# Weight rows of 4 KB, mode groups at given iterations, and the last modes sent to their rows by transfers, in an attention and spectral-mixing kernel

## The chip, the cores and the metric

The kernel runs on one core of one Trainium2 chip. The metric is the device time of one execution in microseconds (us), as the median of several runs. In the profile PE is the matrix engine TensorE (PEld its weight load), DVE is VectorE, ACT is ScalarE, POOL is GpSimd, and SP is SyncE, which here only issues transfers. DMA stands for the core's 16 DMA engines.

## What is computed

The reference has two parts, cut here to what matters (8 batches, 8 heads, 576 positions, head size 64; then 8 x 576 x 512, 64 modes):

```python
def phi(x):                                  # q and k, with w_phi (64 x 128)
    proj = x @ w_phi
    proj = proj - max(abs(proj))
    return concat([exp(proj), exp(-proj)])
kv, z = k_p^T v, sum(k_p)
x = (q_p kv) / (q_p z + 1e-06)               # per batch and head; then [8, 576, 512]

X = rfft(x, axis=1)[:, :64]                  # 64 modes
Yr = Xr @ w_r[m] - Xi @ w_i[m]               # one 512 x 512 pair of matrices per mode
Yi = Xr @ w_i[m] + Xi @ w_r[m]
u = x + irfft(Y, n=576)
out = u + relu(u @ w_ch)
```

w_r and w_i are f32, 64 x 512 x 512 each, 134 MB together. They are by far the largest input.

## The kernel before

**Two stages of work, one stream of weights.** An attention loop runs n = 0 to 33. Its 32 states S[n] are each one pair of heads of one batch (the first eight: one head of two batches). Iteration n does the feature products of state n, the kv product and the quotient of state n-1 (`kv_mm`, `num_mm`, `numer`) and the forward transform of state n-2 (`x_mm`, line 344). A second loop (line 785 on) finishes the modes, and an output phase (line 821 on) adds the inverse transform, the residual and the relu, and stores.

**Mode groups.** The weights come in 32 groups of equal size: 8 groups of 16 modes with 64 of the 512 input rows each (gi < 0 in `groups`, line 108 on), then for each of three further head pairs g = 1 to 3 eight groups of 8 modes with 128 input rows (gi = 0 to 7). `weights(k)` (line 156) issues the transfers of group k from POOL; they cast f32 to bf16 on the way. For gi >= 0 there are two, wr and wi, each 128 partitions by 8 rows of 512 elements, so a row is 2,048 bytes read and 1,024 written. For gi < 0 there are four of 64 partitions. The pool `pw` holds three buffers of each, so group k + 3 is issued once group k has been used (NW = 3).

**Order on POOL.** In an iteration POOL runs, in program order: the transfers of q and k for later states (`load_qk`, odd n), the weights of the next group, then `vscale` (line 266), which multiplies v by exponentials that ACT made (`ee`); in n < 4 vscale comes ahead. POOL also builds `ident_f` at n = 10. Each transfer that POOL issues carries one of eight completion semaphores in turn (110 to 117 in the trace). SP loads v.

**Using a group.** `mode_mm(k)` (line 390) multiplies 16 times: for two parts ri, two parities of the mode and four j it takes 32 columns of `XT`, which holds the transformed x with blocks of zeros beside it, so that even and odd modes land in different rows of one result. `mode_sum` (line 424) adds the result to `Yacc`. In the attention loop group k is used at the end of the iteration, one at most, when n >= after[k] + 2, up to 22 groups (`K_IN_ATTN`). The other ten are used in the second loop.

**The second loop.** Beside the mode groups it makes x W for the output: `flip_x` transposes a pair of x chunks on PE, `times_w` multiplies by `wchb` and ACT copies to `xw`. `plan[k]` says how many such pieces follow group k. From k = 24 (g = 3) the sum `yst` of a group is final. It is transposed to `sY`, and after every second group `by_batch(sY, P)` (line 697) makes, for the 32 rows 32P on, both the spectral rows themselves (yall, `mm_r`) and their product with w_ch (zall, `mm_z`), sorted by batch. Both are halves of the tile `zy`, [row, z or y, batch, 512]. For P < 3 eight copies bring the results to their rows from PSUM. For the last P, batches 0 and 4 are copied directly and the other six go through the tiles `st0` and `st1` and six transfers (lines 730 to 738).

**Output.** Unit u covers two chunks of one batch. `add_xw` and `add_z` sum x W and the inverse transform of zall in `psB`, ACT makes the relu (L762), `spec` sums the inverse transform of yall to the residual in `psA`, and DVE adds the two (L776). Some units get their residual late, added on POOL (L780). The first units are batch 0, then batch 4, then 1, 5 and so on. Unit 0's x W (psB) and residual (psA) are put into PSUM before the last group's result is there.

Every engine works its list in the order written (`tc.manual_schedule`).

Of the kernel before, what the change touches and what calls it, by code (L numbers as in the profile page):

```python
# [20 lines left out]
DMODEL = 512  # L21
# [5 lines left out]
def kernel(  # L27
# [128 lines left out]
    def weights(k):  # L156
        g, gi = groups[k]
        wt = {}
        for ri, w in ((0, moe_w_r), (1, moe_w_i)):
            t = pw.tile([128, 8, DMODEL], BF16, name=f"w{'ri'[ri]}", tag=f"w{ri}")  # L160
            if gi >= 0:
                nc.gpsimd.dma_start(  # L162
                    t, w[8 * gi:8 * gi + 8, g * 128:(g + 1) * 128, :].rearrange("m p e -> p m e"))
            else:
                for x in range(2):
                    mx = 16 * (-1 - gi) + 8 * x
                    nc.gpsimd.dma_start(
                        t[64 * x:64 * x + 64],
                        w[mx:mx + 8, g * 64:(g + 1) * 64, :].rearrange("m p e -> p m e"))
            wt[ri] = t  # L170
        W[k] = wt


# [170 lines left out]
    def x_mm(st):  # L344
# [14 lines left out]
        else:  # L359
            g = st["g"]  # L360
            for c in range(NCH):
                nc.tensor.matmul(
                    psx[:, 0, :, :],
                    lhsT=xs_all[:, st["b"] * NCH + c, g * 128:(g + 1) * 128],
                    rhs=CF4[:, c, :, :],
                    start=(c == 0), stop=(c == NCH - 1),
                )
        for i, b in enumerate(st["bs"] if "bs" in st else (st["b"],)):
# [21 lines left out]
    def mode_mm(k, tag="yr"):  # L390
        g, gi = groups[k]
        XT = XTs[1 - g if k < 8 else g % 2]
        wt = W.pop(k)
# [16 lines left out]
        psY = psum.tile([128, DMODEL], F32, name="psY", tag=tag, bufs=1)  # L410
        for ri in range(2):
            for par in range(2):
                for j in range(4):
                    m = 8 * gi + 2 * j + par
                    c0 = (16, 0, 48, 32)[2 * ri + par]
                    nc.tensor.matmul(  # L416
                        psY[32 * j:32 * j + 32, :],
                        lhsT=XT[:, c0:c0 + 32, m],
                        rhs=wt[ri][:, 2 * j + par, :],
                        start=(par == 0 and ri == 0), stop=(par == 1 and ri == 1),  # L420
# [3 lines left out]
    def mode_sum(k, psY, pb=None):  # L424
# [12 lines left out]
        else:  # L437

            cuts = [0, DMODEL] if k < 31 else [0, DMODEL // 2, DMODEL]
            yst = []  # L440
            for a, b in zip(cuts, cuts[1:]):
                t = pb.tile([128, b - a], BF16, name="yst", tag="yst" if k < 31 else f"yst{a}",
# [86 lines left out]
    with tc.manual_schedule():  # L529
# [25 lines left out]
        for n in range(N + 2):  # L555
# [25 lines left out]
            if n < 4:  # L581
                vscale(cur)
# [304 lines left out]
```

## Time and profile before

| What | Value |
|---|---|
| runs of the kernel before | 455.9, 456.46, 459.7 us; median 456.46 |
| span of the profiled execution | 456.66 us |
| mean granted TensorE clock | 0.883 |
| PE, DVE, ACT, POOL busy | 66%, 64%, 57%, 44% of the span |
| moved by DMA | 97.70 MB counted as written; HBM read 163.64 MB, written 9.44 MB |
| weight transfers, issue to landing (median) | wr 25.8 us, wi 29.4 us for groups 8 to 31 |
| vaug on POOL (L270) | 64 times, 1,155 ns each |
| x_mm (L362), groups of five products | 120 products, 18.7 us busy |
| XT copy on ACT (L369) | 40 times, 391 ns each |
| last weight transfer landed | 414.40 us |
| first output transfer issued | 424.31 us |

How to read it: times are from the span's start. "Busy" is the share in which an engine ran an instruction; a transfer's issue on POOL is not counted there. GB/s counts the bytes written, so a casting transfer reads twice as much. A DMA share over 1 means that packets of one DMA engine overlap. Releasers of waits are inferred. The landing of a transfer is the moment when the last of its 16 engines reported.

### The profile page before, as it was taken

The page shows a single profiled execution, that of the slowest core. Times are in us where ns is not written, and L with a number is a line of the kernel's source. Part 1 is how long each engine was busy: PE and PEld are TensorE (multiplying, and loading weights), DVE is VectorE, ACT ScalarE, POOL GpSimd, SP SyncE. Part 2 cuts the span into 40 slices and gives each one's busy share as a digit, 9 for nine tenths or more (in the row PEclk, how much of TensorE's full clock was granted, in tenths as well). Part 3 has the DMA queues.
Part 4 walks back from the last instruction along what each step waited for, and adds up shares of the span by engine and source line. Part 5 has one row for each costly group of instructions (what it writes and reads, how often), then busy time and mean ns, then how long its engine had stood idle before and what let it go on. Part 6 is the DMA issues. An engine that isn't in the chain of part 4 may idle for free.

```text
span 456.7 us, 11065 instructions
## 1 busy us (share of the span) xinstructions
PE 301.7 (66%) x4637; PEld 197.6 (43%) x4637; DVE 292.0 (64%) x418; ACT 261.8 (57%) x528; POOL 198.8 (44%) x251
## 2 busy tenths in 40 slices
PE   3476776833767677655555544755578878868993
PEld 2355565622555565544333432433344445433341
DVE  6578789844988779876666472776322273653873
ACT  4576887833686877865545452765334455644662
POOL 3956476445563256553435231443021212100993
PEclk9976899876886769998778595999999999998997
DMA  6999999999999999999999999999999999990697
GB/s 179 195 228 222 225 213 226 221 206 216 221 228 217 230 219 222 224 219 229 218 207 217 218 218 218 207 203 207 207 207 207 207 207 207 207 179 11 223 341 299
DMA packets 84417, 97.70 MB, mean 214 GB/s; under 512 B 3152, under 2 KB 77136, under 8 KB 84368
## 3 DMA queue, kind: packets, MB, share of 16 engines
q0 software_dynamic: 75728, 76.75, 101.1%
q1 hardware_dynamic: 8480, 20.19, 12.8%
q8 instruction: 36, 0.59, 0.5%
q14 instruction: 13, 0.11, 0.1%
q10 hardware_dynamic: 160, 0.07, 0.1%
HBM read 163.64 MB, written 9.44 MB: 379 GB/s over the span
## 4 chain that ended last, share of the span: by engine, by line
DMA 34%; issue 24%; DVE 17%; PE 11%; POOL 7%; ACT 3%; SPq 1%; DVEq 0%; POOLq 0%; ACTq 0%
DMA wi<-in_moe_w_i_dram 29%; DVE mkq L233 6%; DMA wr<-in_moe_w_r_dram 4%; DVE xs_all L336 2%; DVE nd L322 2%; DVE tB L315 2%; POOL vaug L270 2%; PE ptr L184 1%; PE psNB L305 1%; ACT AA L240 1%; PE kvz L286 1%; PE psB L753 1%; DVE of L776 1%; SPq L122 1%; POOL wr L162 1%
## 5 line engine op out<-in xcount | busy, mean ns | idle before, releaser
L270 POOL TENSOR_TENSOR vaug<-vn,ee 128x576 bf16<-128x576 f32 x64 | 72.7, 1155 | 63.3 <-ACT ee L255 50.2
L240 ACT ACTIVATE AA<-psT 128x1024 bf16<-128x1024 f32 x64 | 62.0, 1021 | 43.6 <-PE psT L208 43.1
L262 ACT ACTIVATE e<-mkq 64x4 f32<-64x4 f32 (+1 forms) x128 | 26.3, 206 | 61.5 <-DVE mkq L233 59.2
L244 ACT ACTIVATE AA<-psk 128x1024 bf16<-128x1024 f32 x64 | 61.4, 1010 | 0.0
L162 POOL DMA_DIRECT2D wr<-in_moe_w_r_dram x24 | 21.9, 912 | 86.6 <-PE psY L416 77.8
L416 PEld LDWEIGHTS <-XT 128*32 128x32 bf16 x384 | 17.1, 171 | 56.6 <-issue 46.4
L667 ACT CAST xw<-psW 128x1024 bf16<-128x1024 f32 x17 | 17.2, 1013 | 40.5 <-PE psW L665 34.6
L233 DVE TENSOR_REDUCE mkq<-psk 128x8 f32<-128x1024 f32 x32 | 38.8, 1213 | 0.7 <-PE psk L199 0.7
L233 DVE TENSOR_REDUCE mkq<-psq 128x8 f32<-128x1024 f32 x32 | 38.9, 1217 | 0.4 <-PE psq L199 0.4
L435 DVE TENSOR_TENSOR Yacc<-psY,Yacc 128x512 f32<-128x512 f32 x16 | 11.0, 689 | 42.5 <-PE psY L416 42.5
L416 PE MATMUL psY<-wi,XT 128*32 128x512 bf16 x192 | 18.0, 435 | 28.8 <-DMA wi<-in_moe_w_i_dram 28.8
L286 PE MATMUL kvz<-vaug,AA 64*128 64x65 bf16 x1152 | 29.2, 210 | 11.5 <-POOL vaug L275 9.8
L190 DVE COPY kT<-ptr 128x640 bf16<-128x640 bf16 x32 | 15.7, 492 | 32.5 <-PE ptr L184 32.5
L665 PE MATMUL psW<-wchb,sT 128*128 128x512 bf16 x136 | 33.5, 391 | 2.1 <-ACT xw L667 2.1
L315 DVE TENSOR_TENSOR tB<-psNB,e 128x650 f32<-128x650 f32 x32 | 26.7, 833 | 11.2 <-PE psNB L305 10.6
L305 PEld LDWEIGHTS <-AA 128*128 128x128 bf16 x640 | 29.0, 110 | 9.3 <-issue 8.9
L286 PEld LDWEIGHTS <-AA 64*128 64x128 bf16 x1152 | 25.1, 107 | 15.9 <-issue 11.8
L162 POOL DMA_DIRECT2D wi<-in_moe_w_i_dram x24 | 21.1, 880 | 23.8 <-PE psY L416 20.5
L322 DVE TENSOR_TENSOR nd<-psNA,tB 128x650 f32<-128x650 f32 x32 | 26.7, 835 | 4.1 <-DVE tB L315 0.5
L416 PE MATMUL psY<-wr,XT 128*32 128x512 bf16 x192 | 17.0, 424 | 18.0 <-DMA wr<-in_moe_w_r_dram 8.7
L336 DVE TENSOR_TENSOR xs_all<-nd,rden 128x640 bf16<-128x640 f32 x32 | 28.0, 874 | 1.1
L184 PE MATMUL ptr<-ident_b,k 128*128 128x128 bf16 x160 | 17.9, 257 | 14.8 <-DVE qT L190 12.6
(132 smaller groups left out, 705.4 us busy)
## 6 DMA issues: line engine op xcount, KB each, us to landing
wr<-in_moe_w_r_dram POOLq DMA_DIRECT2D x24, 1024.0 KB, 25.8
wi<-in_moe_w_i_dram POOLq DMA_DIRECT2D x24, 1024.0 KB, 29.4
wr<-in_moe_w_r_dram POOLq DMA_DIRECT2D x16, 512.0 KB, 15.9
wi<-in_moe_w_i_dram POOLq DMA_DIRECT2D x16, 512.0 KB, 19.6
out_dram<-of SPq DMA_DIRECT2D x16, 512.0 KB, 3.8
vn<-in_v_dram SPq DMA_DIRECT2D x24, 288.0 KB, 5.8
q<-in_q_dram POOLq DMA_DIRECT2D x12, 288.0 KB, 19.3
k<-in_k_dram POOLq DMA_DIRECT2D x12, 288.0 KB, 20.0
```

The source lines that it names most:

```text
L162: nc.gpsimd.dma_start(t, w[8 * gi:8 * gi + 8, g * 128:(g + 1) * 128, :].rearrange("m p e -> p m e"))
L233: nc.vector.tensor_reduce(out=o, in_=i, axis=AX.X, op=ALU.max, apply_absolute_value=True)
L240: nc.scalar.activation(AA[:, 0, ab, 0:1024].rearrange("f (x j p) -> f j x p", j=2, p=64), st["psT"].rearrange("f j (x p) -> f j x p", p=64 ...
L244: nc.scalar.activation(AA[:, 1, ab, 0:1024].rearrange("p (c j f) -> p j c f", c=4, j=2), st["psk"], ACT.Exp, scale=sc)
L270: nc.gpsimd.tensor_tensor(out=vaug[:, ab, :, 0:64], in0=st["v"], in1=ee[:, ab, :].unsqueeze(2).to_broadcast([128, 9, D_]), op=ALU.mult,)
L286: nc.tensor.matmul(kvz[:, hh, ab * 65:(ab + 1) * 65], lhsT=AA[r, 1, ab, 128 * j:128 * j + 128], rhs=vaug[r, ab, j, :], start=(j == 0), sto ...
L305: nc.tensor.matmul(p[:, hh, 65 * c:65 * c + 65], lhsT=AA[:, 0, ab, x:x + 128], rhs=kvzF[:, hh, ab * 65:(ab + 1) * 65], start=True, stop=True,)
L315: nc.vector.tensor_tensor(out=tB, in0=st["psNB"], in1=e2.unsqueeze(3).to_broadcast([128, 2, NCH, 65]), op=ALU.mult,)
L322: nc.vector.tensor_tensor(out=nd, in0=st["psNA"], in1=st["tB"], op=ALU.add)
L336: nc.vector.tensor_tensor(out=xo, in0=nd[:, :, :, 0:64], in1=rden.to_broadcast([128, 2, NCH, 64]), op=ALU.mult,)
L416: nc.tensor.matmul(psY[32 * j:32 * j + 32, :], lhsT=XT[:, c0:c0 + 32, m], rhs=wt[ri][:, 2 * j + par, :], start=(par == 0 and ri == 0), sto ...
L665: nc.tensor.matmul(ps[:, x, :], lhsT=sT[:, x, dc, :], rhs=wchb[:, dc, :], start=(dc == 0), stop=(dc == 3))
```

## The change

It has six parts.

1. `weights(k)` no longer issues. It puts four halves (wr and wi, two halves of 64 partitions) on a list `due`, and `issue_weights(n)` issues up to n of them: 3 per iteration for n = 9 to 26, 4 in the others, all of them in the second loop. For gi >= 0 a half y holds the modes of parity y, and each partition takes two neighbouring input rows as one run of 4,096 bytes read and 2,048 written. Groups with gi < 0 are transferred as before.
2. To match, `x_mm` for g >= 1 computes even and odd input rows and even and odd modes apart (20 products of 128 columns in place of 5 of 256, and two ACT copies of 64 partitions in place of one of 128), and `mode_mm` takes other columns of XT, again 16 products. `zeros_late` clears two more blocks of each XT on POOL, at n = 9 and 15.
3. From n = 9 `vscale` stands ahead of `load_qk` and of the weights on POOL. `ident_f` is built at n = 6.
4. The groups in the attention loop are used at given iterations `at`, 20 of them in place of 22; `plan` has entries from k = 20.
5. Two x W pieces are kept until group 31, between its wr products and its wi products. Its result is in bank T1.
6. For groups 30 and 31 (gi = 6 and 7) the rows of y and z go to their places by transfers of 16 partitions, seven for each of the two, straight from `yst` and from a copy `z8` of the group's product with w_ch. Batch 0 of the last 32 rows is made by products as before (`first_batch`). The last case of `by_batch` and its st tiles go.

```diff
     def weights(k):
         g, gi = groups[k]
-        wt = {}
+        W[k] = wt = {}
         for ri, w in ((0, moe_w_r), (1, moe_w_i)):
-            t = pw.tile([128, 8, DMODEL], BF16, name=f"w{'ri'[ri]}", tag=f"w{ri}")
-            if gi >= 0:
-                nc.gpsimd.dma_start(
-                    t, w[8 * gi:8 * gi + 8, g * 128:(g + 1) * 128, :].rearrange("m p e -> p m e"))
...
+            for y in range(2):
+                def issue(ri=ri, w=w, y=y):
+                    if y == 0:
+                        wt[ri] = pw.tile([128, 8, DMODEL], BF16, name=f"w{'ri'[ri]}", tag=f"w{ri}")
+                    t = wt[ri][64 * y:64 * y + 64]
+                    if gi >= 0:
+                        nc.gpsimd.dma_start(
+                            t.rearrange("p (m i) e -> p m (i e)", i=2),
+                            w[8 * gi + y:8 * gi + 8:2, g * 128:(g + 1) * 128, :].rearrange(
+                                "m (p i) e -> p m (i e)", i=2))
...
+                due.append((k, issue))
...
+            g, b = st["g"], st["b"]
+            for i in range(2):
+                for c in range(NCH):
+                    for y in range(2):
+                        nc.tensor.matmul(
+                            psx[64 * y:64 * y + 64, 0, :, 32 * i:32 * i + 32],
+                            lhsT=xs_all[:, b * NCH + c, g * 128 + i:(g + 1) * 128:2],
+                            rhs=CF4[:, c, :, y::2],
+                            start=(c == 0), stop=(c == NCH - 1),
+                        )
+            for y in range(2):
+                nc.scalar.copy(
+                    XT[64 * y:64 * y + 64, :, 2 * y:2 * y + 2, b, :],
+                    psx[64 * y:64 * y + 64, 0, :, :].rearrange("d (x y) m -> d x y m", x=2),
...
-                        lhsT=XT[:, c0:c0 + 32, m],
-                        rhs=wt[ri][:, 2 * j + par, :],
+                        lhsT=XT[:, 16 + 32 * ri:48 + 32 * ri, 32 * i + 4 * gi + j],
+                        rhs=wt[ri][:, 2 * j + i, :],
...
+    def zeros_late(i):
+        for z in (16, 48):
+            nc.gpsimd.memset(XTs[i][64:128, z:z + 16, :], 0.0)
...
-    K_IN_ATTN = 22
+    at = [5, 6, 7, 8, 9, 10, 12, 13, 17, 18, 19, 20, 21, 23, 24, 25, 27, 29, 30, 31]
...
+            if 9 <= n < N:
+                vscale(cur)
             if n % 2 == 1 and 5 <= n < N - 5:
                 load_qk((n + 5) // 2)
             while k_in < min(k_out + NW, 2 if n < 3 else 32):
                 weights(k_in)
                 k_in += 1
+            issue_weights(3 if 9 <= n < 27 else 4)
...
-            if cur and n >= 4:
-                vscale(cur)
...
-            if k_out < K_IN_ATTN and n >= after[k_out] + 2:
+            if k_out < len(at) and n == at[k_out]:
...
+    def by_row(all_b, t, gi):
+        for b in (4, 1, 5, 2, 6, 3, 7):
+            (nc.sync if b in (4, 1) else nc.gpsimd).dma_start(
+                all_b[16 * gi:16 * gi + 16, b, :], t[b::8, :])
+
+    def first_batch(sY):
+        cols = [sY[:, dc].rearrange("p g c -> p (g c)")[:, 0::8] for dc in range(4)]
+        ps = psum.tile([128, 2, DMODEL], F32, name="psZY", tag="T0")
+        r = slice(96, 128)
+        for dc in range(4):
+            nc.tensor.matmul(ps[r, 0, :], lhsT=cols[dc], rhs=wchb[:, dc, :],
+                             start=(dc == 0), stop=(dc == 3))
+        for dc in range(4):
+            nc.tensor.matmul(ps[r, 1, dc * 128:(dc + 1) * 128], lhsT=cols[dc], rhs=ident_b,
+                             start=True, stop=True)
+        nc.scalar.copy(zall[r, 0, :], ps[r, 0, :])
+        nc.vector.tensor_copy(yall[r, 0, :], ps[r, 1, :])
+
+    def z_of_group(sY, gi):
+        ps = psum.tile([128, DMODEL], F32, name="psZ", tag="T3" if gi == 6 else "T1")
+        for dc in range(4):
+            nc.tensor.matmul(ps, lhsT=sY[:, dc, gi % 2, :], rhs=wchb[:, dc, :],
+                             start=(dc == 0), stop=(dc == 3))
+        z = pb.tile([128, DMODEL], BF16, name="z8", tag="z8")
+        nc.scalar.copy(z[:, 0:256], ps[:, 0:256])
+        nc.vector.tensor_copy(z[:, 256:512], ps[:, 256:512])
+        by_row(zall, z, gi)
...
-        plan = {22: 3, 23: 3, 24: 2, 25: 2, 26: 2, 27: 1, 28: 2, 29: 1, 30: 1, 31: 0}
+        plan = {20: 3, 21: 3, 22: 2, 23: 2, 24: 1, 25: 1, 26: 1, 27: 1, 28: 1, 29: 1, 30: 1, 31: 0}
...
-            if k == 31:
+            issue_weights()
+            if k < 31:
+                psY = mode_mm(k, "T3")
+            else:
+                psY = mode_mm(k, "T1", ris=(0,))
+                times_w("T2")
+                times_w("T0")
+                add_x(u0)
+                mode_mm(k, ris=(1,), psY=psY)
                 add_xw(u0)
-            yst = mode_sum(k, mode_mm(k, "T3"), pb)
+            yst = mode_sum(k, psY, pb)
             k_out += 1
             if yst is not None:
-                if ahead:
+                if gi >= 6:
+                    by_row(yall, yst, gi)
+                if ahead and k < 30:
                     times_w()
...
+                if gi == 7:
+                    first_batch(sY)
+                if gi >= 6:
+                    z_of_group(sY, gi)
+                elif gi % 2 == 1:
                     by_batch(sY, gi // 2)
-            pieces(plan[k])
+            pieces(plan[k], 1 + (k == 30))
```

## The prediction

> **What bounds the kernel now.** I read four views in this order: the page's 40 slices with its DMA queues, the stretches, the chain of waits, and the timeline from the last weights to the first output.
>
> ```profile
> DMA  6999999999999999999999999999999999990697
> GB/s 179 195 228 222 225 213 226 221 206 216 221 228 217 230 219 222 224 219 229 218 207 217 218 218 218 207 203 207 207 207 207 207 207 207 207 179 11 223 341 299
> ...
> q0 software_dynamic: 75728, 76.75, 101.1%
> ...
> DMA 34%; issue 24%; DVE 17%; PE 11%; POOL 7%; ACT 3%; SPq 1%; DVEq 0%; POOLq 0%; ACTq 0%
> ```
>
> From the second slice to the 35th the DMA engines never fall below nine tenths, and the rate is flat at 207 GB/s once only weights move. GB/s counts bytes written. Weights are read as f32 and written as bf16, so 207 written is 414 read. Nearly everything is POOL's queue q0.
>
> ```profile
> 290.00:320.00 30.00, 19.28 (x350) 12.33 (x348) 20.62 (x32) 19.69 (x45) 12.84 (x15) 1.00 1.24 206
> 320.00:350.00 30.00, 20.34 (x206) 11.87 (x205) 9.64 (x15) 9.44 (x16) 3.56 (x4) 1.00 1.24 207
> ...
> 380.00:405.00 25.00, 19.67 (x264) 11.74 (x256) 13.22 (x16) 13.11 (x14) 3.49 (x4) 1.00 1.24 207
> 409.00:425.00 16.00, 12.50 (x115) 5.72 (x115) 8.31 (x11) 7.50 (x9) 2.19 (x4) 0.89 0.21 41
> 425.00:456.60 31.60, 23.50 (x119) 9.56 (x117) 19.95 (x19) 16.35 (x18) 23.11 (x11) 0.93 0.81 301
> ```
>
> The columns are length, then PE, PEld, DVE, ACT and POOL busy, granted clock, DMA share, GB/s. In 320 to 350 DVE and ACT work a third of the time while DMA stays at 1.24 (packets overlap): the compute engines wait for weights. From 409 DMA drops to 0.21.
>
> ```profile
> 205.84 34.61 DMA wi<-in_moe_w_i_dram
> ...
> 244.92 35.97 DMA wi<-in_moe_w_i_dram
> ...
> 282.35 29.69 DMA wi<-in_moe_w_i_dram
> ```
>
> These pieces of the chain run from a weight transfer's issue to its landing: 30 to 36 us in a full queue. So an attention iteration that waits here costs nothing itself. The time is: start, one saturated stream, and what follows its last byte (landed at 414.40 by the trace's landing records; the fastest of the 16 engines was done at 407.07).
>
> ```profile
> 404.63 0.69 PE L416 MATMUL psY<-wi,XT 128*32 128x512 bf16 x8 [1.16 <-DMA wi<-in_moe_w_i_dram]
> ...
> 410.72 3.22 PE L665 MATMUL psW<-wchb,sT 128*128 128x512 bf16 x8
> ...
> 416.08 0.60 PE L416 MATMUL psY<-wi,XT 128*32 128x512 bf16 x8
> ...
> 419.58 1.00 ACT L718 CAST zy<-psZY 32x1024 bf16<-32x1024 f32 x1 [4.59 <-PE psZY L711]
> ...
> 421.93 1.23 DVE L735 CAST st<-psZY 128x1024 bf16<-128x1024 f32 x1
> ...
> 422.29 2.23 POOL L737 DMA_DIRECT2D zy<-st  x4 [32.96 <-issue]
> ...
> 423.07 2.35 DVE L776 TENSOR_TENSOR of<-psA,of 128x1024 f32<-128x1024 f32 x2
> ```
>
> The last wi matmuls start 1.68 us after their data landed, because PE was in x W and psB. Unit 0's sum starts 6.99 us after those matmuls, behind the 1.23 us cast to st, and unit 2's relu at 424.72, which the chain puts down to zy's transfer. After that PE sets the pace (7 us per batch pair) to 456.66.
>
> **The change, part by part.** The sum stands on this execution's span, 456.66; the median of the runs is 456.46, so I take 0.2 off at the end.
>
> *4 KB rows.* Groups k = 8 to 31 read two 2 KB rows as one; groups 0 to 7 keep theirs. A group takes 2 x 5.06 = 10.12 us (landings at 347.50, 352.56, 357.62), so 24 groups take 242.9 us. A packet occupies its engine 5.06 us / 64 = 79.1 ns. What of that is fixed? By the packet records 1,024 written bytes take 98 ns and the 1,152 of q and k 107 ns (medians), 98.4 and 108.6 (means). So 256 read bytes more cost 9 to 10.2 ns, 2,048 cost 72 to 82, and the fixed part is +7 to -2.5 ns. One packet in place of two saves it once in 158.2 ns: from -10.8 us to +3.8. The output's 4,096-byte stores run at 406 GB/s (439 to 443 us), 2% under 414, which is +5.0 as the upper end. I take 4 ns, nearer to the medians since the means hold collisions with other queues: 2.5%, **-6.1 us**.
>
> The Trainium skill (DMA: Bandwidth & Descriptors, Why small descriptors are slow) gives about 3 cycles per packet; with the 850 MHz of its Specifications that is an estimated 3.5 ns and -5.4 us, and the trace's +7 to -2.5 ns holds it. Against the change, its section iDMA fabric measures a load stream with 4 KiB rows alone at 408.7 GB/s; by that the term would be +3.4 us, and no run here shows such loads yet.
>
> *Four half transfers a group in place of two.* Halves exist already for k below 8: those of k = 6 and 7 land 2.5 us apart (120.53, 123.08, 125.62), half of 5.06, so the stream pays nothing. POOL pays 4 x 0.70 against 2 x 0.90 us, 1.0 us a group, beside DMA. But POOL's eight completion semaphores rotate, so its ninth transfer waits for the first. Eight halves are 20 us of stream: enough to feed it, but POOL waits more. Behind that wait sat vscale, hence the next part.
>
> *vscale ahead of the transfers from n = 9.* vaug (2 x 1.15 + 0.25 us) waits for ee about 5.1 us into the iteration (183.7 in the one that begins at 178.6), so the q, k and weight transfers behind it issue some 7 us later than now. Cover: the queue's depth. It is thinnest before k = 11, whose buffer waits for mode group 8 at n = 17: now wr is issued at 171.72 and the queue's last k lands at 179.63, 7.9 us of cover. Then: group 7 is used as its halves land (131 us, n = 13), four iterations of 7.95 follow, and n = 18's vscale ends at about 173.5 against 178.8: 5.3 us left. Later groups stand likewise, thinner where two iterations lie between uses. A dry spell of 1 or 2 us starves the early engines and not the last, which has a lag of 6 us to catch up. I take **+1.0 us**, from 0 to +15 (second rival).
>
> *20 groups at given iterations, twelve later.* This moves waits, not bytes: the attention slows less on landings and the loop after it holds two groups more. Cover: in 320 to 405 PE is busy 0.68 to 0.84 of the time. Zero.
>
> *x_mm in 20 products and two copies.* Five of 256 columns take 0.56 to 0.71 us; 20 of 128 columns, 64 wide, by the q transposes (10 in 0.68) 1.36: +0.7 us on PE. psq then ends at 186.3 instead of 185.58, and its absmax on DVE starts at 187.09 anyway. ACT gets one more XT copy, 0.39 us, before a wait of 1.77 (waits: ACT e on mkq, 59.2 us in 32). Both hidden. Uncovered they would cost 1.1 us in each of 24 iterations, beside a full DMA queue. If the stride-2 reads halved PE's speed, psq would end 0.5 us after its time. The half memsets (four, 1 us each by the 0.20 to 0.27 of 128x128) and ident_f at n = 6 lie on POOL with that cover: zero; ident_f moves out of a 7.2 us wait at n = 10 that the stream hides too.
>
> *x W pieces kept for the end.* After wr's half of group 31, PE does two times_w (1.90 each, 3.22 when the clock drops as at 410.72) and add_x (0.4 to 0.6): 4.4 to 7.0 us inside a gap of 5.07 between wr and wi (409.33, 414.40). Then wi's matmuls start 0 to 2.7 us after landing, where they now start 1.68 after: -1.7 to +1.0, I take **-0.7**.
>
> *Last sixteen modes by rows.* From the wi matmuls (time 0) yst, transposes and sY stay: 2.1 us. Then 8 products for batch 0 replace 64: four of 512 columns one after another (0.9 to 1.1) and four small, 3.2. ACT and DVE copy 32x512 in 0.6 each (a 128x512 of L388 takes 0.59) instead of 32x1024 in 1.00 and 1.22, and both st casts (1.01, 1.23) go. In their place come 4 products and two half copies of z, 0.4 each: relu 4.7, unit 0's sum 5.7 against 6.99. z's rows for batch 4, now copied on the chip, become a new wait: they leave SP at 4.65 and land 2.15 later (as zy: 421.69 to 423.84), at 6.8. Unit 2's products and relu follow at 7.4 against 8.64 (424.72), so the output's chain runs 1.2 us earlier. 28 row transfers replace 6; on SP two and two of 0.6; on POOL ten for the last group, 0.55 each, done at 7.4, and its first late add starts at 8. If POOL holds back group 30's rows until wi lands (semaphores), 1.7 us move in there. **-1.2**, from -1.6 to +1.5.
>
> Sum: -6.1 + 1.0 - 0.7 - 1.2 = -7.0; 456.66 - 7.0 - 0.2 = **449.5 us**.
>
> **The rivals.**
> 1. *4 KB packets carry no more per second.* For it: stores of that size at 406. Against: a flat 79.1 ns at 2 KB with medians that leave a fixed part. Time: 449.5 + 6.1 = 455.6; with the upper end, 460.6.
> 2. *The queue runs dry in the attention (the other side).* Place: k = 11 and after. If an iteration grows by d over 7.95, eight iterations (n = 10 to 17) put k = 11's issue 8d later; dry from d = 5.3 / 8 = 0.66. From n = 18 to 31 fourteen more iterations add up to 14d, less some 8 us that waits for landings hold now. At d = 1.2: 4.3 + 8.8 = 13 us, 449.5 + 13 = 462.5; it decides against the change from d of about 1.1 (past 461). For it: issues 7 us later, half the depth, the loop of e, exps, kvzF, tB, nd, xs_all, mkq fills its 7.9 us. Against: x_mm and the copy lie outside that loop with 0.8 and 1.4 us to spare.
> 3. *More than forecast.* The medians' 7 ns: -10.8 instead of -6.1, 444.8.
> 4. *PE late at the end:* both times_w at the low clock and z behind: 449.5 + 1.7 + 1.5 = 452.7.
>
> **How the numbers follow.** Forecast (446 to 451.8) 0.48; first rival 0.20; second 0.15; third 0.10; fourth 0.07. Within 1% of 456.46, about what a measurement of this kernel can tell from no change, means 451.9 to 461.0. Faster: 0.48 + 0.10 = 0.58. Same: 0.20 + 0.07 = 0.27. Slower: 0.15. The range 442 to 461.5 takes in both ends of the packet price and leaves out the second rival and a little of the third.
>
> **What would show it.** Weight-only stretches at 210 to 213 GB/s instead of 207, and half transfers landing 2.45 to 2.48 us apart, bear out the rate; 207 is the first rival. A digit under 9 in the DMA row between slices 15 and 30, or POOL waiting on DMA with DVE and PE behind vaug, is the second. Landing to unit 0's sum (now 8.67 us) should be 5.7 to 7. Wrong would be attention iterations over 8.6 us without a landing to wait for.

## The result, and the profile after

| | before | after |
|---|---|---|
| median of 14 runs each | 456.03 us | **459.99 us** (457.38 to 463.57) |
| ratio of the runs, 95% interval | | 1.007 (1.0047 to 1.0092) |
| span of the profiled execution | 456.66; taken again 455.36 | 458.40 |
| time of that execution | taken again 457.15 | 460.18 |
| mean granted TensorE clock | 0.883; taken again 0.878 | 0.861 |

The change makes the kernel 0.7% slower, 3 to 4 us. Ratios leave out runs in the chip's slower state, of which there is one here, among the ten of e11, whose median without it is 456.07 us and not 456.6. An execution's time is some 1.8 us over its span (457.15 and 455.36, 460.18 and 458.40). By that, as an estimate, the execution of the first profile took about 458.5, 2 us over the median; the prediction's "0.2 off" took span and median for the same thing, which leaves its difference of 7 us as it was. Below, both profiles of the kernel before stand beside the one after; the one taken again is called the second.

The page after: slices, the POOL queue, the chain.

```profile
DMA  6999999999999999999999999899999999990597
GB/s 182 194 229 223 223 207 220 227 217 225 222 221 221 223 231 214 224 223 215 220 219 213 228 217 209 156 200 210 212 211 211 211 211 211 211 195 16 205 346 285
...
q0 software_dynamic: 52432, 76.82, 93.7%
...
DMA 35%; PE 22%; DVE 19%; ACT 11%; POOL 5%; issue 5%; SPq 1%; DVEq 0%; ACTq 0%; POOLq 0%
```

Where only weights move the rate is 211 in place of 207, 2% more, and the packets of q0 took 93.7% of the engines' span in place of 101.1%. But slice 26 (286 to 298 us) has 156, and its neighbours 209 and 200. A slice is 11.46 us, so (2 + 55 + 11) / 211 x 11.46 = 3.7 us of stream are missing there; that is nearly all that 4 KB rows bring in. And PE's share of the chain has gone from 11% to 22%.

The stretches (length, then PE, PEld, DVE, ACT, POOL busy, granted clock, DMA share, GB/s):

```profile
320.00:350.00 30.00, 24.35 (x190) 13.18 (x192) 7.88 (x12) 13.30 (x14) 7.39 (x12) 1.00 1.12 211
380.00:405.00 25.00, 16.89 (x229) 9.39 (x222) 12.46 (x15) 9.15 (x10) 3.67 (x6) 0.93 1.12 211
409.00:425.00 16.00, 12.88 (x62) 5.22 (x63) 6.18 (x10) 4.68 (x7) 5.50 (x12) 0.78 0.23 49
425.00:458.40 33.40, 24.59 (x122) 10.09 (x122) 21.16 (x20) 17.22 (x19) 24.27 (x14) 0.93 0.76 286
```

The last two have moved: 409 to 425 ran at a clock of 0.78 in place of 0.89. The timeline from the last weights to the first outputs shows how PE comes late:

```profile
409.45 2.46 DVE L748 CAST zy<-psZY 32x1024 bf16<-32x1024 f32 x2
...
410.71 0.48 POOL L758 DMA_DIRECT2D zy<-z  x1 [1.95 <-DMA wi<-in_moe_w_i_dram]
...
411.97 1.09 PE L435 MATMUL psY<-wr,XT 128*32 128x512 bf16 x8 [3.26 <-DVE zy L748]
...
412.99 5.13 PE L695 MATMUL psW<-wchb,sT 128*128 128x512 bf16 x16
...
417.96 0.59 PE L811 MATMUL psA<-xs_all,ident_p 128*128 128x512 bf16 x2
...
418.48 0.68 PE L435 MATMUL psY<-wi,XT 128*32 128x512 bf16 x8
...
424.18 1.22 DVE L819 TENSOR_TENSOR of<-psA,of 128x1024 f32<-128x1024 f32 x1 [0.66 <-ACT of L805]
...
425.91 1.02 ACT L805 ACTIVATE of<-psB 128x1024 f32<-128x1024 f32 x1 [0.32 <-PE psB L803]
```

The trace's landing records have the last wr half in at 407.74 and the last wi half at 413.01. The wr products of group 31 start only at 411.97: their result goes to bank T1, which holds results of an earlier `by_batch` until DVE has copied them out (L748, to 411.91). Behind them, in program order, PE has sixteen products of x W, 5.13 us, and the residual. The last wi products therefore start at 418.48, **5.47 us after their data** (1.68 and 2.28 in the two profiles before). As a sum: 4.23 us from the landing of wr to its products, 6.51 us of PE's work to 418.48, less the 5.27 between the two landings. From there on the change does what it should: unit 0's sum comes 5.70 us later (6.99 before), unit 2's relu 7.43 (8.64 before).

The time, in spans:

| | first before | second before | after | after less first / second |
|---|---|---|---|---|
| last wi half landed | 414.40 | 412.58 | 413.01 | -1.4 / +0.4 |
| to the wi products | 1.68 | 2.28 | 5.47 | +3.8 / +3.2 |
| to the end | 40.58 | 40.50 | 39.92 | -0.7 / -0.6 |
| span | 456.66 | 455.36 | 458.40 | +1.7 / +3.0 |

### The profile page after: what moved, and what is told of

It is laid out like the page before. It is cut to its first block, busy times and chain, and to the rows that moved or that the text cites. A ratio compares the mean times of both kernels' runs of the same rounds, so it can differ in the third digit from the quotient of the medians.

```text
span 458.4 us, 11786 instructions
## 1 busy us (share of the span) xinstructions
PE 317.2 (69%) x4933; PEld 207.4 (45%) x4949; DVE 291.4 (64%) x419; ACT 269.9 (59%) x553; POOL 226.0 (49%) x319
## 3 DMA queue, kind: packets, MB, share of 16 engines
q0 software_dynamic: 52432, 76.82, 93.7%
## 4 chain that ended last, share of the span: by engine, by line
DMA 35%; PE 22%; DVE 19%; ACT 11%; POOL 5%; issue 5%; SPq 1%; DVEq 0%; ACTq 0%; POOLq 0%
DMA wi<-in_moe_w_i_dram 30%; DVE mkq L245 6%; DMA wr<-in_moe_w_r_dram 4%; PE psW L695 3%; DVE xs_all L348 3%; DVE nd L334 3%; ACT AA L252 3%; PE psY L435 3%; ACT e L274 2%; ACT AA L256 2%; POOL vaug L282 1%; PE psNB L317 1%; DVE tB L327 1%; PE psA L817 1%; PE kvz L298 1%
## 5 line engine op out<-in xcount | busy, mean ns | idle before, releaser
L166 POOL DMA_DIRECT2D wr<-in_moe_w_r_dram x48 | 30.1, 633 | 61.5 <-PE psY L435 46.3
L166 POOL DMA_DIRECT2D wi<-in_moe_w_i_dram x48 | 30.3, 638 | 19.7 <-DMA wi<-in_moe_w_i_dram 10.4
L695 PE MATMUL psW<-wchb,sT 128*128 128x512 bf16 x130 | 35.5, 416 | 3.7 <-ACT xw L697 3.4
L220 PE MATMUL psT<-qT,w 64*128 64x512 bf16 x64 | 14.8, 451 | 21.8 <-DVE mkq L245 21.7
L435 PE MATMUL psY<-wr,XT 128*32 128x512 bf16 x192 | 19.1, 476 | 14.1 <-ACT AA L260 5.9
```

The costliest lines, as they stand in the source:

```text
L166: nc.gpsimd.dma_start(t.rearrange("p (m i) e -> p m (i e)", i=2), w[8 * gi + y:8 * gi + 8:2, g * 128:(g + 1) * 128, :].rearrange("m (p i) ...
L435: nc.tensor.matmul(psY[32 * j:32 * j + 32, :], lhsT=XT[:, 16 + 32 * ri:48 + 32 * ri, 32 * i + 4 * gi + j], rhs=wt[ri][:, 2 * j + i, :], st ...
L695: nc.tensor.matmul(ps[:, x, :], lhsT=sT[:, x, dc, :], rhs=wchb[:, dc, :], start=(dc == 0), stop=(dc == 3))
```

## The experiments

All kernels compute the whole output. Ratios are to the kernel before on the same chip, with 95% intervals. "Landed" is the landing of the last wi half, "late" the time from there to the last wi products.

**Theory.** 4 KB rows do speed up the stream; twice as many POOL transfers over the same eight completion semaphores shorten the queue in time and give that back; and PE is late at the end. **Rival:** the stream bounds as before, and PE's lateness is absorbed.

### The end

*e1_pieces_first:* the same work on PE, in another order.

```diff
-                psY = mode_mm(k, "T1", ris=(0,))
                 times_w("T2")
                 times_w("T0")
                 add_x(u0)
+                psY = mode_mm(k, "T1", ris=(0,))
```

> The changed kernel, with both kept x W pieces and unit 0's residual put ahead of group 31's wr products on PE instead of between wr and wi. First theory (PE is late at the end: group 31's wr products wait 3.26 us for bank T1, whose copies stand on DVE, and the two pieces run after them at a low clock, so that wi's products start 5.5 us after their data landed): the pieces fill the wait, wi's products start 0.5 to 1.5 us after landing, and the time falls by 3.5 to 4.5 us from 460.0 to about 456. Rival (what costs is the stream, dry in the attention, and the end is hidden): the time stays at 459 to 461.

Measured: 455.29 us, ratio 0.9975 (0.9952 to 0.9998). Landed 412.63, 1.76 late.

```profile
407.41 6.10 PE L695 MATMUL psW<-wchb,sT 128*128 128x512 bf16 x16
...
413.88 0.68 PE L435 MATMUL psY<-wr,XT 128*32 128x512 bf16 x8
...
414.39 0.60 PE L435 MATMUL psY<-wi,XT 128*32 128x512 bf16 x8
```

The pieces now run while the bank is still being read. One line in another place is worth 4.7 us of the medians (459.99 to 455.29; by the ratios 1.007 to 0.9975), and the change is no longer slower than the kernel before. What is left of the lateness goes with the speed of the pieces: here they ran at a granted clock of 0.50 up to 412.44 (last section), while the profiles of e10, e11 and e12, with the same end at a clock of 1.0, are 0.04 us late.

*p_tail_only:* the kernel before (2 KB rows, whole transfers) with the new end alone: kept pieces, T1, rows sent by transfers; 22 groups in the attention loop and whole transfers of 2 KB rows stay.

```diff
+            if k < 31:
+                psY = mode_mm(k, "T3")
+            else:
+                psY = mode_mm(k, "T1", ris=(0,))
+                times_w("T2")
+                times_w("T0")
+                add_x(u0)
+                mode_mm(k, ris=(1,), psY=psY)
...
+                if gi >= 6:
+                    z_of_group(sY, gi)
```

> The kernel before with the end alone: two x W pieces kept, group 31 split into wr and wi with its result in T1, rows sent by transfers, 17 pieces planned from group 22; weights, x_mm, POOL order and iterations of use as before. First theory (PE late at the end costs 3.8 us, the work after it saves 1): 458 to 460, 2 to 4 us over before. Rival (the end gains as forecast and the loss is in the stream): 454 to 455.5.

Measured: 461.65 us, 1.0107 (1.0078 to 1.0136). That is beyond the range of either theory, on the side of the first. The same picture with the old stream:

```profile
415.27 1.11 PE L417 MATMUL psY<-wr,XT 128*32 128x512 bf16 x8 [1.68 <-DVE zy L717]
416.31 4.59 PE L664 MATMUL psW<-wchb,sT 128*128 128x512 bf16 x16
...
421.26 0.69 PE L417 MATMUL psY<-wi,XT 128*32 128x512 bf16 x8
```

The last wr half landed at 407.70, the last wi half at 412.92, so the wi products are 8.3 us late. The lateness is there without the new rows and without the new schedule: it belongs to the new end.

### The stream

*p_rows_only:* the kernel before with 4 KB halves and what goes with them (`x_mm`, `mode_mm`, `zeros_late`); old order on POOL, old iterations, old end.

```diff
-                nc.gpsimd.dma_start(
-                    t, w[8 * gi:8 * gi + 8, g * 128:(g + 1) * 128, :].rearrange("m p e -> p m e"))
+                    nc.gpsimd.dma_start(
+                        t.rearrange("p (m i) e -> p m (i e)", i=2),
+                        w[8 * gi + y:8 * gi + 8:2, g * 128:(g + 1) * 128, :].rearrange(
+                            "m (p i) e -> p m (i e)", i=2))
```

> The kernel before with the 4 KB rows alone: four half transfers a group for all groups, the x_mm, mode_mm and zero blocks that go with them; order on POOL, iterations of use, plan and end as before. First theory (the rate rises from 207 to 211 GB/s written and nothing else is lost): 24 groups at 9.94 instead of 10.12 us, 4 us less than before's 456.0, 451.5 to 453. Rival (eight semaphores hold only two groups of halves, POOL waits and vscale behind it stretches the attention, the queue then runs dry): 456 to 462, with POOL waiting on DMA landings and vaug late.

Measured: 466.17 us, 1.0235 (1.0192 to 1.0277). The rival was right, and the loss lies beyond its range. The GB/s row of its page:

```profile
GB/s 184 196 229 216 220 183 217 230 205 229 207 226 217 233 200 113 220 231 211 226 217 221 222 221 221 222 212 211 211 188 187 207 210 211 211 179 1 216 340 290
```

Slice 16 (175 to 186 us) has 113: the queue is dry, and PE waited 43.2 us for vaug in all (9.7 and 9.8 in the profiles before). *e3_halves_2kb* separates number from size: the kernel before, its rows still 2 KB, with only this:

```diff
-                nc.gpsimd.dma_start(
-                    t, w[8 * gi:8 * gi + 8, g * 128:(g + 1) * 128, :].rearrange("m p e -> p m e"))
+                for y in range(2):
+                    nc.gpsimd.dma_start(
+                        t[64 * y:64 * y + 64],
+                        w[8 * gi:8 * gi + 8, g * 128 + 64 * y:g * 128 + 64 * y + 64, :].rearrange(
+                            "m p e -> p m e"))
```

> The kernel before with each weight transfer of groups 8 to 31 cut into two halves of 64 partitions, rows still 2 KB, nothing else changed. First theory (the rows-only kernel lost 9.6 us because eight semaphores then hold 20 us of queue in place of 35, POOL waits and the queue runs dry before group 11): the same loss without the rate's gain, 462 to 468, with the landing of group 11 5 to 8 us later than in the kernel before. Rival (x_mm's 20 products, the second XT copy and the memsets stretched the attention): 456 to 458.

Measured: 467.83 us, 1.027 (1.022 to 1.0321): 10.7 us for cutting the same bytes into twice as many transfers. Against the second profile before, the last wi half lands 8.8 us later (421.42), and PE is 4.55 us late behind it, 2.3 more. POOL's timeline around the issue of group 10 in this kernel, and then in the second profile of the kernel before:

```profile
142.24 0.68 POOL L163 DMA_DIRECT2D wr<-in_moe_w_r_dram  x1 [1.72 <-DMA wi<-in_moe_w_i_dram]
145.03 0.68 POOL L163 DMA_DIRECT2D wi<-in_moe_w_i_dram  x1 [2.10 <-DMA wr<-in_moe_w_r_dram]
147.32 0.68 POOL L163 DMA_DIRECT2D wi<-in_moe_w_i_dram  x1 [1.62 <-DMA wr<-in_moe_w_r_dram]
148.02 2.27 POOL L273 TENSOR_TENSOR vaug<-vn,ee 128x576 bf16<-128x576 f32 x2
```

```profile
130.64 0.88 POOL L162 DMA_DIRECT2D wr<-in_moe_w_r_dram  x1 [0.79 <-PE psY L403]
131.51 0.88 POOL L162 DMA_DIRECT2D wi<-in_moe_w_i_dram  x1
134.72 2.26 POOL L270 TENSOR_TENSOR vaug<-vn,ee 128x576 bf16<-128x576 f32 x2 [2.33 <-ACT ee L255]
```

Before, two issues follow each other and vaug waits only for its exponentials. With halves each issue waits 1.6 to 2.1 us for the landing of an earlier transfer; with its own 0.68 us that is about one half's time on the stream (2.53 us). The earlier transfer is the one eight issues back: POOL's issues use the eight semaphores in strict turn, and in the traces of e3 and of the kernels before and after none starts less than 0.28 us after the landing of the last transfer with its semaphore. In e3 65 of 161 start within 0.6 us of it, in the first profile before 26 of 113. vaug, with the whole attention behind it, starts with no wait left: it stood behind the issues. From the vaug before it to this one 16.0 us pass in place of 8.7, group 11 is issued at 180.5 in place of 170.7, and the stream runs dry (120 GB/s in the slice from 175 to 187 us). The loss is there with either size of rows.

*e2_weights_ahead_n27* puts the weights ahead of vscale again for the last iterations, since POOL after showed the dry spell of slice 26 (start, length):

```profile
286.02 2.27 POOL L282 TENSOR_TENSOR vaug<-vn,ee 128x576 bf16<-128x576 f32 x2 [7.74 <-ACT ee L267]
288.23 0.26 POOL L287 CAST vaug<-ee 128x18 bf16<-128x18 f32 x1
288.37 1.27 POOL L166 DMA_DIRECT2D wr<-in_moe_w_r_dram  x2
```

Group 17 was used up by 282.72, but group 20's transfers stand behind vaug and leave at 288.37. By the landing records the fastest DMA engine had finished the queue at 286.18, and its next half, due 2.49 us later, came at 292.95: 4.3 us dry.

```diff
-            if 9 <= n < N:
+            if 9 <= n < 27:
                 vscale(cur)
...
-            if 4 <= n < 9:
+            if 4 <= n < 9 or 27 <= n < N:
                 vscale(cur)
```

> The changed kernel, with weights issued ahead of vscale on POOL again from n = 27. First theory of the stream (the dip to 156 GB/s at 286 to 297 us is a dry queue: group 20 can only be issued at 288.4, behind vscale of n = 30, 6 us after its buffer came free): the dip goes, the landings after it come 1.5 to 3 us earlier, and the time falls to 457 to 458.5. Rival (the dip starves only the early engines and the last engine sets the end): the dip goes, the last landing and the time stay within 1 us of 413 and 460.

Measured: 461.78 us, 1.0112 (1.0067 to 1.0157), slower than either theory said. The dip at 286 is gone and group 20 has landed at 299.89 in place of 302.07, as the first theory had it, but other dips stand from 311 to 345 (193, 195, 197 GB/s): PE was 14 to 16 us behind with groups 20 to 23, so their buffers came free late. Landed 412.95, nothing gained. A dry spell closed at one place opened at the next limit. The end is still that of the changed kernel, and PE is 7.23 us late here.

*e5_pieces_first_22_groups:* e1 with 22 groups in the attention loop (n = 5 to 12 and 17 to 30), four halves per iteration, and the 17 x W pieces planned from group 22 on.

```diff
-    at = [5, 6, 7, 8, 9, 10, 12, 13, 17, 18, 19, 20, 21, 23, 24, 25, 27, 29, 30, 31]
+    at = list(range(5, 13)) + list(range(17, 31))
...
-            issue_weights(3 if 9 <= n < 27 else 4)
+            issue_weights(4)
...
-        plan = {20: 3, 21: 3, 22: 2, 23: 2, 24: 1, 25: 1, 26: 1, 27: 1, 28: 1, 29: 1, 30: 1, 31: 0}
+        plan = {22: 3, 23: 3, 24: 2, 25: 2, 26: 2, 27: 2, 28: 1, 29: 1, 30: 1, 31: 0}
```

> The changed kernel with the kept pieces first and the attention using 22 groups at the iterations of before (n = 5 to 12 and 17 to 30), up to four half transfers an iteration. First theory (using groups 16 to 19 at n = 25 to 28 frees buffers earlier, no dip at 286, but PE waits more often for landings): last landing 1 to 2 us earlier than 412.6, 453.5 to 455. Rival (the given iterations were what kept POOL and PE from waiting): 457 to 461.

Measured: 466.61 us, 1.0207 (1.0175 to 1.024), 11.3 us over e1; group 11 issued at 181.4, as late as in e3. But the loss is made up otherwise. The last wi half lands at 415.92, 3.3 us later than in e1; the larger part is PE, 10.91 us late. The attention ends later (last vaug at 321.0 us, 296.3 in e1), and PE is still 6.7 us behind with group 30, for which it waits in e1. Three runs take the cap, the first two changes of the list, and the place of vscale, one by one from e1 (455.29):

*e10_vscale_behind_weights:* vscale behind the weights in all iterations from n = 4.

```diff
-            if 9 <= n < N:
-                vscale(cur)
...
-            if 4 <= n < 9:
+            if 4 <= n < N:
                 vscale(cur)
```

> The version with both pieces ahead of the wr products (455.3 us), with vscale behind the weights' issues again in every iteration from n = 4, as in the kernel before; half transfers, the cap of 3 per iteration and the given iterations stay. First theory (twice as many transfers over eight semaphores make POOL wait, and what stands behind POOL's wait is the attention itself): PE kvz waits on POOL vaug for 15 us or more in all, issues of groups 10 to 14 come late, a dry spell appears near 180 us, and the time is 459 to 464 us. Rival (the given iterations alone do the work, the place of vscale is worth nothing): 454.5 to 456.5 us, with POOL vaug waits of PE below 10 us.

Measured: 456.3 us, 0.9986 (0.9958 to 1.0014). My theory failed here: the order is worth nothing that can be told. PE does wait for vaug (14.2 us, between what the two theories said), but group 11 is issued at 172.1 and at 172.4 in e1. With vscale ahead POOL waits 91.6 us for ee with the transfers behind it, with vscale behind 24.0 us; that the two orders cancel is my reading, the time shows only that they do not differ. It also limits e3: halves, with vscale behind them, do not cost e3's 10.7 us by themselves; they do so with the old iterations.

*e11_no_cap:* up to four halves per iteration.

```diff
-            issue_weights(3 if 9 <= n < 27 else 4)
+            issue_weights(4)
```

> The version with both pieces ahead of the wr products (455.3 us), with up to four halves issued per iteration throughout in place of three from n = 9 to 26. Groups stay at their given iterations. The version with 22 groups and four halves took 466.6 us, and its group 11 was issued at 181.4 in place of 172.4. First theory (four halves in one iteration run into the eight completion semaphores, POOL stops, and the attention stops behind it): an attention iteration of 11 us or more before n = 17, group 11 issued after 176 us, time 458 to 463 us. Rival (it is the iterations at which groups are used, not the cap): group 11 issued at 171 to 174 us and 454.5 to 456.5 us.

Measured: 456.6 us, 0.9986 (0.9952 to 1.0021), group 11 issued at 173.0: the rival again, no difference that can be told.

*e12_groups_6_7_earlier:*

```diff
-    at = [5, 6, 7, 8, 9, 10, 12, 13, 17, 18, 19, 20, 21, 23, 24, 25, 27, 29, 30, 31]
+    at = [5, 6, 7, 8, 9, 10, 11, 12, 17, 18, 19, 20, 21, 23, 24, 25, 27, 29, 30, 31]
```

> The same version (455.3 us) with only groups 6 and 7 used one iteration earlier, at n = 11 and 12 as the version with 22 groups does, in place of 12 and 13; the cap of three halves stays. First theory (a group used before its data are there stops PE, and with it the attention, and every later group comes late): an iteration of 12 us or more near n = 11, group 11 issued after 176 us, time 458 to 463 us. Rival (the wait only changes its place, since group 7's data land at 131 us either way): group 11 issued at 171 to 175 us and 454.5 to 456.5 us.

Measured: 461.18 us, 1.0126 (1.0082 to 1.017). Two numbers cost 5.9 us of the medians (four runs; the profiled one, 458.19, is the fastest of them). PE at group 6 in e12, and then in e1:

```profile
112.26 0.47 PE L423 MATMUL psY<-wr,XT 64*32 64x512 bf16 x7 [0.17 <-DMA wr<-in_moe_w_r_dram]
115.00 0.37 PE L423 MATMUL psY<-wi,XT 64*32 64x512 bf16 x1 [2.28 <-DMA wi<-in_moe_w_i_dram]
118.11 0.69 PE L423 MATMUL psY<-wi,XT 64*32 64x512 bf16 x7 [2.74 <-DMA wi<-in_moe_w_i_dram]
```

```profile
120.03 0.48 PE L423 MATMUL psY<-wr,XT 64*32 64x512 bf16 x8
120.31 0.41 PE L423 MATMUL psY<-wi,XT 64*32 64x512 bf16 x8
```

Used at n = 11, PE stands and waits for each half, and the attention behind it; used at n = 12, the data are there. Group 11 is then issued at 179.4 in place of 172.4, the slices around 171 to 194 carry 173 and 206 GB/s, and the last weights land at 416.62 in place of 412.63. The stream never gets that back.

### Put together

*e4_pieces_first_ahead_n27_even_plan:* e1 and e2 with the x W pieces spread evenly (two after each of groups 20 to 25), so that buffers come free in time.

```diff
-        plan = {20: 3, 21: 3, 22: 2, 23: 2, 24: 1, 25: 1, 26: 1, 27: 1, 28: 1, 29: 1, 30: 1, 31: 0}
+        plan = {20: 2, 21: 2, 22: 2, 23: 2, 24: 2, 25: 2, 26: 1, 27: 1, 28: 1, 29: 1, 30: 1, 31: 0}
```

> The changed kernel with the kept pieces first, weights ahead of vscale from n = 27, and the 17 x W pieces spread 2 a group over groups 20 to 25 and 1 over 26 to 30 in place of 3, 3, 2, 2 and ones. First theory (in the second loop PE uses groups 20 to 23 up to 15 us after they landed, so their buffers come free late and the queue runs dry there once the earlier dip is gone): no stretch under 205 GB/s from 280 on, last landing 410 to 411, 452 to 453.5. Rival (the last engine alone sets the end and takes no gain): 455 to 456, as with the pieces first alone.

Measured: 454.47 us, 0.994 (0.9916 to 0.9963). Landed 411.83, 1.75 late: better than before, and not as good as the first theory. One slice (317 to 329 us) still has 187 GB/s.

*e7_one_piece_kept:* e4 with one x W piece kept in place of two.

```diff
                 times_w("T2")
-                times_w("T0")
                 add_x(u0)
...
-                if ahead and k < 30:
+                if ahead and k < 31:
                     times_w()
...
-            pieces(plan[k], 1 + (k == 30))
+            pieces(plan[k], 1)
```

> The fourth combined version (both pieces and the residual ahead of the last wr products, weights ahead of vscale again from n = 27, x W pieces spread evenly) with one x W piece kept in place of two; the other is made beside group 30, as in the kernel before. In the version with two, the sixteen products of x W took 4.84 us (407.87 to 412.71) and the last wi products began at 413.58, 1.75 us after their data. First theory (PE is late because of the second piece): eight products take at most 3.2 us, the wi products start 0.3 to 0.8 us after the landing, and the time falls by about 1.2 us from 454.5 to 453.3, ratio to before about 0.992. Rival (the piece moved to group 30 delays that group's rows and the last landing is what it is): 454.5 or more, wi products still 1.5 us or more after the landing.

Measured: **452.74 us**, 0.9924 (0.9892 to 0.9955), faster than both kernels. The end of PE:

```profile
407.80 1.90 PE L695 MATMUL psW<-wchb,sT 128*128 128x512 bf16 x8 [0.79 <-DVE sT L687]
...
410.29 0.67 PE L435 MATMUL psY<-wr,XT 128*32 128x512 bf16 x8 [0.16 <-DVE zy L748]
411.81 0.69 PE L435 MATMUL psY<-wi,XT 128*32 128x512 bf16 x8 [0.84 <-DMA zy<-z]
```

The wi products start 0.05 us after their data landed (411.76; the releaser named in the brackets is inferred). Against e4 the trace gains 1.6 us of span (453.28 to 451.7); the intervals of the two overlap, so the runs alone do not part them. Nor does the trace show that the second piece was the cause: in e4 the pieces ran at a granted clock of 0.50 up to 410.34, in e7 at 1.0; and e10, e11 and e12 keep both pieces and are 0.04 us late, at 1.0.

*e6_before_again:* the kernel before, for a second profile.

> The kernel before, profiled once more. Both theories expect its span at 454 to 455 (median of the runs less some 1.8 us around the span), the last weights landed at 411 to 413 rather than 414.4, and the same order of events; if it is again 456.7, the two profiles can be compared as they stand.

Measured: 457.15 us, span 455.36, landed 412.58, 2.28 late, a flat 207 to 208 GB/s from 290 us on.

## Why the prediction was wrong, step by step

It said 449.5 us and faster; the change is slower. The gains it named are real; two losses, one put at +1.0 and one not seen, were larger. That 459.99 lies inside its range of 442 to 461.5 is luck: the range was drawn for the price of a packet, and the end and the queue used it up.

- *4 KB rows, -6.1.* The mechanism is right, the size about two thirds: 211 against 207 GB/s, a half every 2.485 us, a group in 9.94 us against 10.12. That is 24 x 0.18 = -4.3 us, and 2.8 ns saved per pair of packets where I took 4. The first rival (no more per second) is out. The Trainium skill (DMA: Bandwidth & Descriptors, Why small descriptors are slow), by my estimate 3.5 ns from its 3 cycles, was nearer than my choice; the 408.7 GB/s of its section iDMA fabric, for a stream of 4 KiB rows issued from SP, is no limit for these casting loads from POOL, which read 422. The stores from 439 to 443 us run at 408 GB/s by the view of that stretch, not 406, which would have put the upper end of this term at +3.8.
- *Four half transfers, "enough to feed it", and vscale ahead, +1.0.* This failed. The stream's end moved by -1.4 or +0.4 us against the two profiles before, so the queue gave back 3 to 5 us against the 4.3. By the last landings, 1.3 to 2.5 of it were lost by group 19, 1.2 to 1.8 at group 20, and 0.4 after. The second rival had the right mechanism (halved depth, a dry queue) and the wrong place: group 11 was issued at 173.8 (forecast 173.5; 171.7 and 170.7 before), and the spell came at 286, where group 20 stood behind vaug. What the halves cost uncovered is e3's 10.7 us, 8.8 of them at the last landing. The Trainium skill (DMA: Bandwidth & Descriptors, Rules for kernel authors) says of two transfers to disjoint partition halves "Don't bother" and advises one 128-partition transfer, because both use the same engines; e3 agrees with the advice, for another reason, the semaphores; the page names no price.
- *20 groups at given iterations, zero.* Wrong in this kernel: it is what pays for the halves. Two groups used one iteration early cost 4.0 us at the last landing (e12). The old 22 with four halves an iteration cost 11 us (e5): 3.3 at the last landing and most of the rest because PE comes late. I priced the groups moved to the second loop and not the waits that the new list avoids.
- *x_mm, the copies, the memsets, zero.* Borne out as far as the trace goes: attention iterations without a wait take 7.9 to 8.1 us before and after, and the 20 products, which I counted at 1.36 us, took 0.88 on average (21.0 us in 24 iterations).
- *x W pieces kept for the end, -0.7.* The step that turned the sign: +3.2 to +3.8. I summed PE's work between the two landings (4.4 to 7.0 us) as if it began when wr landed. It began 4.23 us later, at 411.97, because the result's bank had a reader on DVE first. I counted durations and did not ask what bank T1 held. Of the work itself the fourth rival (PE late, both pieces at the low clock) was right: they ran at 0.50 for 3.1 of their 5.13 us. It named the right place at less than half the price, 1.7 us over the forecast's -0.7 where it came to 3.9 to 4.5.
- *Last modes by rows, -1.2.* Right on the points named: 5.70 and 7.43 us, forecast 5.7 and 7.4. To the end it is -0.6 to -0.7; the rest of the output gave back the difference. Group 30's rows on POOL do wait for landings (at 410.71 behind a wi transfer, 1.95 us), as I feared, without delaying the end.

By its parts the sum is the last column of the table: stream -1.4 or +0.4 (rate and queue together), PE late +3.8 or +3.2, the rows -0.7 or -0.6, so +1.7 or +3.0 us. What stays open: where the queue lost its 1.3 to 2.5 us before group 19, what the second x W piece costs apart from the clock, and whether 4 KB rows in one transfer of 128 partitions would keep the whole 4.3; such a kernel was not tried.

## What to carry to other kernels

Count a queue's depth in transfers and not only in bytes: cutting transfers in two halves it wherever a fixed number of completions is in flight, and the engine that waits to issue takes everything behind it along. When work is put into a gap before the last data, ask what its result tile still holds and who reads that, and place first what has its operands and its bank free. In a saturated stream a wait of the compute engines is free only while the next issue is not late: one late buffer early on (e12) was still missing 4 us at the end. And it is free only while the work left over still fits ahead of the last data: in e5 PE was 10.91 us late.

## What the runs showed of the hardware

- In the two profiles before, where the queue was always full, the last of the 16 DMA engines reports 4.65 to 7.64 us after the first for groups 20 to 31 (406.84 to 412.58 for the last in the second). After, it is 4.2 us at group 19, 1.6 at group 20, behind the dry spell, and 1.1 to 2.3 from there on (410.99 to 413.01 for the last). So a spell that starves the fast engines costs the last landing less than its length: across the 4.3 us at 286 the first landing of after falls behind the second profile before by 4.1 us more (0.9 at group 19, 5.0 at group 20), the last landing by 1.6 more (0.4, 2.0).
- Sixteen x W products took 3.62 us in e10, at a granted clock of 1.0, and 6.10 in e1. After, by stretches (columns as above):

```profile
404.00:408.00 4.00, 2.09 (x11) 0.98 (x13) 1.22 (x3) 1.15 (x2) 2.46 (x5) 0.73 1.13 212
408.00:412.00 4.00, 0.74 (x11) 0.60 (x10) 3.14 (x3) 1.23 (x2) 0.97 (x2) 0.50 0.95 188
412.00:416.00 4.00, 4.00 (x16) 1.28 (x16) 0.00 (x0) 0.00 (x0) 1.43 (x3) 0.50 0.08 21
416.00:418.50 2.50, 2.50 (x16) 1.00 (x14) 0.00 (x0) 1.35 (x2) 0.00 (x0) 0.99 0.00 0
```

The granted clock fell to 0.50 at 405.83 by the trace's clock records, 2.9 us before PE began to wait for the bank (408.71), and came back at 416.07. Up to there the products ran at half speed: 1.09 us for 0.68 on the wr ones, 5.13 for 3.62 on the x W ones, which ran at full speed again for their last 2 us; 1.9 us in all. The wait did not set this off: in e1, which has no such wait, the clock was at 0.50 from 405.61 to 412.44. Whether the wait made it last longer is not shown. The Trainium skill (TensorE: Matmul & The Clock Gate, Part 1: The HAM clock gate) states the rule of half rate after an idle window of some 3.4 us and full rate after a busy one. The trace agrees on the length, since 10.24 us at 0.50 are three times 3.41, and on the way back, since PE was busy for all of the last 3.41 us; but the fall came behind 3.41 us in which PE was not idle, busy for 1.51.

- A 4 KB packet occupied its DMA engine 173 ns by the packet records (median), a 2 KB one 98 ns. The records overlap, so two of 98 less one of 173 is not what a merged pair saves; the landings give 2.8 ns.
